# Multiplying the first dense layer once per token pair (k, S-k), with the sum and the difference formed on Vector

## The chip, the core and the metric

The kernel runs on one core of a Trainium2 chip. The metric is the device time of one execution in microseconds; the median of three executions of the kernel before is 3000.6 us (3000.43 to 3002.52). The engines are TensorE (PE in the profile, its weight loads PEld), Vector (DVE), Scalar (ACT), GpSimd (POOL) and Sync (SP). Data are float32; the two weight matrices arrive as 64-bit floats and are converted on Vector.

## The reference

```python
# x: (8, 3008, 256)   w_in: (256, 2048)   w_out: (2048, 256)
X = np.fft.fft(np.fft.fft(x, axis=1), axis=2).real     # over the sequence, then over d
x2 = X.reshape(8 * 3008, 256)
h = x2 @ w_in
g = h * np.clip(h + 3.0, 0.0, 6.0) / 6.0
out = g @ w_out                                         # (24064, 256)
```

## The kernel before

The sequence transform of length S = 3008 is split as 47 x 64 (N1, N2). Since x is real, only the residues k1 = 0..23 (NK1 = 24) are computed: the cosine part of a token k equals that of token S-k, the sine part has the opposite sign. Along d, x is first folded into sums x[d] + x[D-d] (columns 0 to D/2) and differences (the other columns), and the last product over d is multiplied into w_in once (fold_w_in, L268), so that h is a product of 256 rows: 128 of the cosine kind, 128 of the sine kind.

Batches go in four pairs. For a pair, eight rounds of load_x (L90, issued by GpSimd), fold (L95, three Vector instructions) and stage1 (L104, four calls a round: one product of 512 columns and one of two columns, which repairs column D/2 among the sine columns; Scalar copies the result out) write an intermediate to DRAM. load_g (L124) brings it back in pieces of eight k1 for one batch, and stage2 (L132, 16 passes of 64 columns a call, then a Vector copy) makes q, whose columns are tokens.

The dense layers run over chunks of up to 8 x 64 = 512 tokens of one batch (chunks_of, L152): 12 chunks a pair, namely for each batch three with the tokens k and three with their partners S-k (the last of these has 7 x 64 = 448). For the partners the same q is read backwards, and the sine block of the weights is the negated copy W1m1. Each chunk has 16 blocks of 128 hidden columns; a chunk and a block make one step, 4 x 12 x 16 = 768 steps. In a step mlp1 (L159) makes h by two products of 512 columns added in PSUM, Scalar makes t (L170), Vector the gate a (L172); mlp2 (L175) multiplies the four tiles of 128 tokens of a with w_out, 256 columns each, adding up in PSUM over the 16 blocks. After the last block Scalar copies each tile and Sync stores it in pieces of 64 tokens.

The order of the instructions is written by hand. mlp1 runs two steps ahead of mlp2 (AHEAD = 2, L333). What belongs to the next chunks and the next pair (load_x, fold, stage1, load_g, stage2, and in the first chunk the conversion of w_out) is placed by beside (L303) into slots of chunk and block; the slot's work is issued ahead of that step's mlp1 and mlp2. In each engine's queue the order is that of issue. PSUM has eight banks: two for stage1 and stage2 (ps_d), two for h (ps_h), four for the accumulators (ps_a), of which a chunk uses two.

Before the loop stand the first pair's eight rounds (L278), with the conversion of w_in and fold_w_in between them, the first batch's load_g and stage2, and two conversions of w_out (eight Vector instructions each, L230 to L237).

Of the kernel before, what the change touches and what calls it, by code (L numbers as in the profile page):

```python
# [27 lines left out]
def kernel(  # L28
# [37 lines left out]
    ps_h = ctx.enter_context(tc.tile_pool(name="ps_h", bufs=2, space=PSUM))  # L66
# [3 lines left out]
    out_k = out.rearrange("(b k2 k1) d -> b k1 k2 d", b=B, k1=N1)  # L70
# [3 lines left out]
    F = consts.tile([PR, 2, PZ], F32, name="F")  # L74
    T = consts.tile([P, 2, NK1, N2], F32, name="T")
    C = consts.tile([P, 2, D], F32, name="C")
    W1p = consts.tile([P, 2, FF], F32, name="W1p")
    W1m1 = consts.tile([P, FF], F32, name="W1m1")
    W2 = consts.tile([P, NFC, D], F32, name="W2")
    half = consts.tile([P, 1], F32, name="half")  # L80
    sign = consts.tile([P, 1], F32, name="sign")

    class Pair:
        def __init__(self, p):
            self.p = p
            self.x, self.y, self.z = {}, {}, {}
            self.zd = None
            self.g, self.q = {}, {}
# [6 lines left out]
    def fold(pr, c):  # L95
        xt = pr.x.pop(c)
        y = ypool.tile([PR, XC, D], F32, tag="y", name="y")
        lo, hi = xt[:, :, 1:P], xt[:, :, D - 1:P:-1]
        nc.vector.tensor_tensor(y[:, :, 1:P], lo, hi, op=AL.add)  # L99
        nc.vector.tensor_tensor(y[:, :, P + 1:D], lo, hi, op=AL.subtract)  # L100
        nc.vector.tensor_copy(y[:, :, 0:P + 1:P], xt[:, :, 0:P + 1:P])  # L101
        pr.y[c] = y
# [21 lines left out]
    def load_g(pr, b, kc):  # L124
        g = gpool.tile([P, KC, D], F32, tag="g", name="g")
        nc.gpsimd.dma_start(  # L126
            out=g[:],
            in_=pr.zd[b].rearrange("k c n d -> (c n) k d")[:, kc * KC:(kc + 1) * KC, :],
        )
        pr.g[b, kc] = g  # L130

    def stage2(pr, b, kc, i):  # L132
        if kc == 0 and i == 0:
            pr.q[b] = qpool.tile([P, 2, NK1, N2], F32, tag="q", name="q")
        g = pr.g[b, kc]
        ps = ps_d.tile([P, 2, 4, N2], F32, tag="d", name="ps2")
        for u in range(4):
            k1 = kc * KC + 4 * i + u
            for blk in range(2):
                nc.tensor.matmul(ps[:, blk, u], g[:, 4 * i + u, blk * P:(blk + 1) * P], T[:, blk, k1],  # L140
                                 start=True, stop=True)
        k0 = kc * KC + 4 * i
        nc.vector.tensor_copy(pr.q[b][:, :, k0:k0 + 4, :], ps[:])  # L143

    class Chunk:
        def __init__(self, pr, b, sg, k0, k1):
            self.pr, self.b, self.sg, self.k0, self.n = pr, b, sg, k0, k1 - k0
            self.nt = self.n * N2
            self.tiles = [(t, min(P, self.nt - t)) for t in range(0, self.nt, P)]
            self.a, self.acc = {}, {}  # L150

    def chunks_of(pr):  # L152
        for b in range(2):
            for sg in (1, -1):
                first = 0 if sg > 0 else 1
                for k0 in range(first, NK1, KC):
                    yield Chunk(pr, b, sg, k0, min(k0 + KC, NK1))

    def mlp1(ch, fc):  # L159
        q = ch.pr.q[ch.b]  # L160
        ps = ps_h.tile([P, TB], F32, tag="h", name="h")
        h = ps[:, 0:ch.nt]
# [6 lines left out]
        t = tpool.tile([P, TB], F32, tag="t", name="t")  # L169
        nc.scalar.activation(t[:, 0:ch.nt], h, AF.Relu, bias=half[:], scale=1.0 / 6.0)  # L170
        a = apool.tile([P, TB], F32, tag="a", name="a")
        nc.vector.scalar_tensor_tensor(a[:, 0:ch.nt], t[:, 0:ch.nt], 1.0, h, op0=AL.min, op1=AL.mult)  # L172
        ch.a[fc] = a

    def mlp2(ch, fc):  # L175
        a = ch.a.pop(fc)
        for i, (t0, n) in enumerate(ch.tiles):
# [3 lines left out]
            nc.tensor.matmul(ch.acc[i // 2][0:n, i % 2], a[:, t0:t0 + n], W2[:, fc, :],  # L181
                             start=(fc == 0 and i % 2 == 0), stop=(fc == NFC - 1), skip_group_check=True)
        if fc == NFC - 1:
            for i, (t0, n) in enumerate(ch.tiles):
                acc = ch.acc[i // 2]
                o = opool.tile([P, D], F32, tag="o", name="o")
                nc.scalar.copy(o[0:n], acc[0:n, i % 2])  # L187
                for j in range(n // N2):
                    k1 = ch.k0 + (t0 + j * N2) // N2
                    rows = out_k[2 * ch.pr.p + ch.b]  # L190
                    dst = rows[k1 if ch.sg > 0 else N1 - k1]
                    nc.sync.dma_start(out=dst, in_=o[j * N2:(j + 1) * N2])
# [9 lines left out]
    # The weights' pieces, [P, 512] each: a 64-bit one comes as pairs of 32-bit words, of  # L202
    # which the float32 is made here.
# [61 lines left out]
    nc.vector.memset(sign[:], -1.0)  # L265
    nc.vector.memset(sign[0:1], 1.0)

    def fold_w_in(n):  # L268
        cs = slice(n * 512, (n + 1) * 512)
        for blk in range(2):  # L270
            ps = ps_h.tile([P, 512], F32, tag="h", name="wps")
# [3 lines left out]
            nc.scalar.copy(W1p[:, blk, cs], ps[:])  # L275
        nc.vector.tensor_scalar(W1m1[:, cs], W1p[:, 1, cs], sign[:], None, op0=AL.mult)

    for c in range(NXC):  # L278
        if c + 2 < NXC:
            load_x(first, c + 2)  # L280
        fold(first, c)
# [9 lines left out]
    for kc in range(NKC):  # L291
        load_g(first, 0, kc)
        for i in range(KC // 4):
            stage2(first, 0, kc, i)
# [4 lines left out]
    # what runs beside the second part: slots of (chunk of the pair, f block)  # L299
    chunks = [list(chunks_of(pr)) for pr in pairs]  # L300
    NCK = len(chunks[0])

    def beside(p):  # L303
# [11 lines left out]
        for kc in range(NKC):  # L315
            put(kc, 0, load_g, cur, 1, kc)
            for i in range(KC // 4):
                put(kc + 1, 4 + 6 * i, stage2, cur, 1, kc, i)
# [83 lines left out]
```

## Time and profile before

| | |
|---|---|
| median of three runs | 3000.6 us |
| span of the profiled execution (first to last instruction) | 2998.8 us |
| TensorE busy | 2944.5 us (98%) |
| Vector busy | 692.9 us (23%) |
| Scalar busy | 663.4 us (22%) |
| GpSimd busy | 38.6 us (1%) |
| mean granted TensorE clock | 0.985 |

The profiled execution's own time is its span and what lies around it; the median of the runs is 1.8 us above that span. In the trace each float32 product appears as two passes, each with its own weight load, so a step's two products of 512 columns are four rows and its four products of 256 columns are eight. A matmul's row is longer than the distance to the next one because matmuls overlap; the distance from start to start is the time that counts. A granted clock of 1.00 is 2.4 GHz, half of it 1.2 GHz.

### The profile page before, as it was taken

What the parts mean: (1) busy time and instruction counts of PE and PEld (TensorE: products, weight loads), DVE (VectorE), ACT (ScalarE), POOL (GpSimd) and SP (SyncE); (2) the same over time, 40 slices, a digit from 0 to 9 for tenths busy, and PEclk for the clock granted to TensorE, in tenths of its full rate; (3) what the DMA queues carried; (4) which work ended last, traced back from release to release, by engine and by line L of the source; (5) the groups of instructions that cost most, each with busy time, mean ns of one, the idle gap of its engine ahead of it and who ended that gap; (6) DMA issues with size and microseconds to landing.
All of it is one profiled execution on the core that took longest, in us unless ns stands there. A gap on an engine that the chain in (4) does not pass through costs nothing.

```text
span 2998.8 us, 25017 instructions
## 1 busy us (share of the span) xinstructions
PE 2944.5 (98%) x10528; PEld 1896.6 (63%) x10528; DVE 692.9 (23%) x1047; ACT 663.4 (22%) x1097; POOL 38.6 (1%) x60
## 2 busy tenths in 40 slices
PE   6899999999999999999999999999999999999999
PEld 2556665666656666566666666566675666666665
DVE  4362222222212222122221222222121222112111
ACT  1122222222222222222212222222212222222221
POOL 0000000000000000000000000000000000000000
PEclk8699999999999999999999999999999999999999
DMA  6422111001200211002020211110111000000000
GB/s 190 150 62 63 28 28 40 23 18 50 69 11 8 69 33 45 17 18 59 26 56 7 60 39 28 28 28 25 46 36 27 8 21 8 15 7 8 14 8 14
DMA packets 47728, 111.53 MB, mean 37 GB/s; under 512 B 7778, under 2 KB 32192, under 8 KB 41408
## 3 DMA queue, kind: packets, MB, share of 16 engines
q1 hardware_dynamic: 37360, 58.56, 7.4%
q0 software_dynamic: 10112, 49.81, 5.7%
q8 instruction: 82, 1.34, 0.2%
q10 hardware_dynamic: 144, 1.57, 0.2%
q14 instruction: 30, 0.25, 0.0%
HBM read 60.10 MB, written 49.81 MB: 37 GB/s over the span
## 4 chain that ended last, share of the span: by engine, by line
PE 97%; DMA 1%; DVE 1%; issue 0%; ACT 0%; SPq 0%; ACTq 0%; POOLq 0%
PE acc L181 45%; PE h L168 44%; PE ps L113 4%; PE ps L140 3%; DMA st<-in_moe_w_in_dram 1%; PE wps L273 1%; DMA g<-zd 0%; PE ps L114 0%; DMA st<-in_moe_w_out_dram 0%; DVE y L99 0%; DVE y L100 0%; DVE ex L236 0%; DVE frac L232 0%; ACT W1p L275 0%; DVE top L230 0%
## 5 line engine op out<-in xcount | busy, mean ns | idle before, releaser
L181 PE MATMUL acc<-W,a 128*128 128x256 f32 (+1 forms) x6144 | 1470.9, 380 | 0.0
L181 PEld LDWEIGHTS acc<-W,a 128*128 128x128 f32 (+1 forms) x6144 | 1143.8, 188 | 509.2 <-issue 396.5
L168 PE MATMUL h<-q,W1p 128*128 128x512 f32 (+1 forms) x2304 | 1124.7, 597 | 5.5 <-DVE a L172 5.5
L172 DVE SCALAR_TENSOR_TENSOR a<-t,h 128x512 f32<-128x512 f32 (+1 forms) x768 | 519.6, 677 | 2116.9 <-ACT t L170 2116.9
L170 ACT ACTIVATE t<-h,half 128x512 f32<-128x512 f32 (+1 forms) x768 | 521.0, 678 | 2002.3 <-PE h L168 2002.3
L168 PEld LDWEIGHTS h<-q,W1p 128*128 128x128 f32 x2304 | 419.3, 190 | 262.1 <-issue 223.4
L168 PE MATMUL h<-q,W1m 128*128 128x512 f32 (+1 forms) x768 | 378.5, 574 | 0.0
L168 PEld LDWEIGHTS h<-q,W1m 128*128 128x128 f32 x768 | 145.9, 190 | 170.0 <-issue 170.0
L113 PE MATMUL ps<-y,F 94*96 94x512 f32 x256 | 159.1, 708 | 32.7 <-DMA F<-in_c_stage_dram 18.4
L116 ACT COPY z<-ps 96x512 f32<-96x512 f32 x128 | 74.4, 581 | 284.5 <-PE ps L114 284.5
L140 PEld LDWEIGHTS ps<-T,g 128*128 128x128 f32 x768 | 102.3, 209 | 12.8 <-issue 10.6
L140 PE MATMUL ps<-T,g 128*128 128x64 f32 x768 | 100.5, 290 | 9.6 <-issue 9.3
L114 PEld LDWEIGHTS ps<-y,F 94*96 94x96 f32 x256 | 48.4, 189 | 85.1 <-issue 85.1
L113 PEld LDWEIGHTS ps<-y,F 94*96 94x96 f32 x256 | 42.6, 187 | 45.7 <-issue 39.8
L187 ACT COPY o<-acc 128x256 f32<-128x256 f32 x192 | 62.0, 375 | 24.6 <-PE acc L181 24.6
L143 DVE COPY q<-ps 128x512 f32<-128x512 f32 x48 | 33.2, 692 | 112.1 <-PE ps L140 112.1
L126 POOL DMA_DIRECT2D g<-zd x24 | 21.4, 892 | 1670.1 <-PE ps L140 958.7
L99 DVE TENSOR_TENSOR y<-xt 94x1016 f32<-94x1016 f32 x32 | 38.6, 1205 | 9.8 <-DMA xt<-in_x_dram 9.8
L100 DVE TENSOR_TENSOR y<-xt 94x1016 f32<-94x1016 f32 x32 | 38.6, 1206 | 0.0
L114 PE MATMUL ps<-y,F 94*96 94x2 f32 x256 | 35.7, 209 | 0.0
L92 POOL DMA_DIRECT2D xt<-in_x_dram x32 | 17.1, 536 | 705.4 <-DVE y L101 704.6
L273 PE MATMUL wps<-w_in,C 128*128 128x512 f32 x32 | 22.5, 867 | 0.0
(21 smaller groups left out, 90.5 us busy)
## 6 DMA issues: line engine op xcount, KB each, us to landing
zd<-z SPq DMA_DIRECT2D x32, 768.0 KB, 4.3
g<-zd POOLq DMA_DIRECT2D x24, 1024.0 KB, 6.7
xt<-in_x_dram POOLq DMA_DIRECT2D x32, 752.0 KB, 7.9
out_dram<-o SPq DMA_DIRECT2D x376, 64.0 KB, 2.0
st<-in_moe_w_in_dram SPq DMA_DIRECT2D x8, 512.0 KB, 6.7
st<-in_moe_w_out_dram SPq DMA_DIRECT2D x8, 512.0 KB, 6.4
T<-in_c_stage_dram ACTq DMA_DIRECT2D x1, 1536.0 KB, 8.6
C<-in_c_dim_dram SPq DMA_DIRECT2D x1, 256.0 KB, 17.8
```

The lines of the kernel that those rows point to most:

```text
L99: nc.vector.tensor_tensor(y[:, :, 1:P], lo, hi, op=AL.add)
L100: nc.vector.tensor_tensor(y[:, :, P + 1:D], lo, hi, op=AL.subtract)
L113: nc.tensor.matmul(ps[0:PZ], F[:, 0], y[:, 2 * i:2 * i + 2, :], start=True, stop=True)
L114: nc.tensor.matmul(ps[0:PZ, :, P:P + 1], F[:, 1], y[:, 2 * i:2 * i + 2, P:P + 1], start=True, stop=True)
L116: nc.scalar.copy(z[:, 2 * i:2 * i + 2, :], ps[0:PZ])
L140: nc.tensor.matmul(ps[:, blk, u], g[:, 4 * i + u, blk * P:(blk + 1) * P], T[:, blk, k1], start=True, stop=True)
L168: nc.tensor.matmul(h, w, qc, start=(blk == 0), stop=(blk == 1))
L170: nc.scalar.activation(t[:, 0:ch.nt], h, AF.Relu, bias=half[:], scale=1.0 / 6.0)
L172: nc.vector.scalar_tensor_tensor(a[:, 0:ch.nt], t[:, 0:ch.nt], 1.0, h, op0=AL.min, op1=AL.mult)
L181: nc.tensor.matmul(ch.acc[i // 2][0:n, i % 2], a[:, t0:t0 + n], W2[:, fc, :], start=(fc == 0 and i % 2 == 0), stop=(fc == NFC - 1), skip_g ...
L187: nc.scalar.copy(o[0:n], acc[0:n, i % 2])
L273: nc.tensor.matmul(ps[:], C[:, i, blk * P:(blk + 1) * P], w_in[n, i][0][:], start=(i == 0), stop=(i == 1))
```

## The change

- The pairs of tokens k and S-k are computed together. mlp1 makes u (the cosine part) and v (the sine part) in two banks of PSUM, one product each. Vector forms s = u + (column D/2's term), then h0 = s + v for the tokens k and h1 = s - v, written backwards, for the tokens S-k. Scalar makes t for both, and Vector gates both in a function of its own (gate), which is issued after the next step's mlp1.
- Column D/2 of the folded data leaves the matrix products: its row of weights is kept as WN, its transform qn is made with a Vector product (stage2n_mul) and a TensorE product with a matrix of ones, which sums over partitions and leaves the sum in all of them (stage2n_sum); s adds WN times qn. In exchange the two-column product of stage1 goes, and fold_w_in gets eight products of one column for each of its four calls.
- A chunk is four k1 of both batches of the pair, so 6 chunks a pair and 384 steps; each has eight tiles of 128 tokens in mlp2 (seven in the last chunk of a pair). The k1 are taken in the order 1..23, 0.
- PSUM: u and v have one bank each; fold_w_in uses ps_d; a chunk uses all four banks of ps_a.
- The folds beside the loop run on GpSimd, in two parts; the copies of stage2 move from Vector to Scalar; x has two buffers instead of three, and before the loop the load of round c+2 is issued after the fold of round c. Only the first chunk's q is made before the loop. Two tiles are copied and stored together.

```diff
-        nc.tensor.matmul(ps[0:PZ], F[:, 0], y[:, 2 * i:2 * i + 2, :], start=True, stop=True)
-        nc.tensor.matmul(ps[0:PZ, :, P:P + 1], F[:, 1], y[:, 2 * i:2 * i + 2, P:P + 1],
-                         start=True, stop=True)
+        nc.tensor.matmul(ps[0:PZ], F[:], y[:, 2 * i:2 * i + 2, :], start=True, stop=True)
...
+    def stage2(pr, ck, i):
+        if i == 0:
+            pr.q[ck] = qpool.tile([P, 2, KC, N2], F32, tag="q", name="q")
+        g = pr.g[ck]
+        ps = ps_d.tile([P, 2, 4, N2], F32, tag="d", name="ps2")
+        for u in range(4):
+            kk, b = 2 * i + u // 2, u % 2
+            for blk in range(2):
+                nc.tensor.matmul(ps[:, blk, u], g[:, b, kk, blk * P:(blk + 1) * P],
+                                 T[:, blk, ck * KK + kk], start=True, stop=True)
+        nc.scalar.copy(pr.q[ck][:, :, 4 * i:4 * i + 4, :], ps[:])
+    def stage2n_mul(pr, ck):
+        m = spool.tile([P, KK, 2, N2], F32, tag="m", name="m")
+        t0 = T[:, 0, ck * KK:(ck + 1) * KK, :].unsqueeze(2).to_broadcast([P, KK, 2, N2])
+        gn = pr.g[ck][:, :, :, P:P + 1].rearrange("p b k o -> p k b o").to_broadcast([P, KK, 2, N2])
+        nc.vector.tensor_tensor(m[:], t0, gn, op=AL.mult)
+        pr.pr[ck] = m
+    def stage2n_sum(pr, ck):
+        m = pr.pr.pop(ck)
+        ps = ps_d.tile([P, TB], F32, tag="d", name="ps3")
+        nc.tensor.matmul(ps[:], ones[:], m[:].rearrange("p k b n -> p (k b n)"), start=True, stop=True)
+        pr.qn[ck] = qpool.tile([P, TB], F32, tag="qn", name="qn")
+        nc.scalar.copy(pr.qn[ck][:], ps[:])
...
-        ps = ps_h.tile([P, TB], F32, tag="h", name="h")
-        for blk in range(2):
-            w = W1m1[:, fs] if blk and ch.sg < 0 else W1p[:, blk, fs]
-            qc = q[:, blk, ch.k0:ch.k0 + ch.n, ::ch.sg]
-            nc.tensor.matmul(h, w, qc, start=(blk == 0), stop=(blk == 1))
-        nc.scalar.activation(t[:, 0:ch.nt], h, AF.Relu, bias=half[:], scale=1.0 / 6.0)
-        nc.vector.scalar_tensor_tensor(a[:, 0:ch.nt], t[:, 0:ch.nt], 1.0, h, op0=AL.min, op1=AL.mult)
+        u = ps_h.tile([P, TB], F32, tag="u", name="u")
+        v = ps_h.tile([P, TB], F32, tag="v", name="v")
+        nc.tensor.matmul(u[:], W1[:, 0, fs], q[:, 0], start=True, stop=True)
+        nc.tensor.matmul(v[:], W1[:, 1, fs], q[:, 1], start=True, stop=True)
+        s = spool.tile([P, KC, N2], F32, tag="s", name="s")
+        h = hpool.tile([P, 2, KC, N2], F32, tag="h", name="h")
+        t = hpool.tile([P, 2, KC, N2], F32, tag="t", name="t")
+        nc.vector.scalar_tensor_tensor(s[:].rearrange("p k n -> p (k n)"), qn[:], WN[:, fc:fc + 1], u[:],
+                                       op0=AL.mult, op1=AL.add)
+        nc.vector.tensor_tensor(h[:, 0], s[:], v3, op=AL.add)
+        nc.vector.tensor_tensor(h[:, 1, 0:nm, ::-1], s[:, 0:nm], v3[:, 0:nm], op=AL.subtract)
+        for sg, n in ((0, KC), (1, nm)):
+            nc.scalar.activation(t[:, sg, 0:n], h[:, sg, 0:n], AF.Relu, bias=half[:], scale=1.0 / 6.0)
+    def gate(ch, fc):
+        a = apool.tile([P, 2, KC, N2], F32, tag="a", name="a")
+        for sg, n in ((0, KC), (1, ch.nm)):
+            nc.vector.scalar_tensor_tensor(a[:, sg, 0:n], t[:, sg, 0:n], 1.0, h[:, sg, 0:n],
+                                           op0=AL.min, op1=AL.mult)
...
+            put(at_ck, 1, stage2n_mul, pr, ck)
+            for i in range(2):
+                put(at_ck, 3 + 4 * i, stage2, pr, ck, i)
+            put(at_ck, 11, stage2n_sum, pr, ck)
...
+                a0 = 8 * c
+                put(a0 // NFC, a0 % NFC, load_x, nx, c)
+                put((a0 + 3) // NFC, (a0 + 3) % NFC, fold, nx, c, 0, nc.gpsimd)
+                put((a0 + 4) // NFC, (a0 + 4) % NFC, fold, nx, c, 1, nc.gpsimd)
...
         if s + AHEAD < len(steps):
-            p1, ck1, fc1 = steps[s + AHEAD]
-            mlp1(chunks[p1][ck1], fc1)
-        mlp2(chunks[p][ck], fc)
+            mlp1(*chunk(s + AHEAD))
+        if s + 1 < len(steps):
+            gate(*chunk(s + 1))
+        mlp2(*chunk(s))
```

## Rows read from the trace of the kernel before

**Rows 1.** The page's busy times: engine, us, share, instructions.

```profile
PE 2944.5 (98%) x10528; PEld 1896.6 (63%) x10528; DVE 692.9 (23%) x1047; ACT 663.4 (22%) x1097; POOL 38.6 (1%) x60
```

**Rows 2.** Stretches: length, busy us of PE, PEld, DVE, ACT, POOL; clock, DMA share, GB/s.

```profile
18.36:115.80 97.44, 83.00 (x160) 35.57 (x160) 49.42 (x88) 22.72 (x40) 2.05 (x4) 0.74 0.51 144
...
160.00:2992.40 2832.40, 2832.40 (x10261) 1836.98 (x10259) 623.83 (x922) 636.79 (x1052) 28.44 (x41) 1.00 0.11 29
```

**Rows 3.** Timeline of a full step: start, length, engine, line, what, idle before.

```profile
2801.00 1.88 PE L168 MATMUL h<-q,W1p 128*128 128x512 f32 x4
...
2802.72 1.89 PE L181 MATMUL acc<-W,a 128*128 128x256 f32 x8
...
2802.92 0.69 ACT L170 ACTIVATE t<-h,half 128x512 f32<-128x512 f32 x1 [2.75 <-PE h L168]
2803.64 0.69 DVE L172 SCALAR_TENSOR_TENSOR a<-t,h 128x512 f32<-128x512 f32 x1 [2.76 <-ACT t L170]
...
2811.33 1.02 PE L168 MATMUL h<-q,W1p 128*128 128x512 f32 x2
```

**Rows 4.** Timeline, two steps of 448 tokens.

```profile
2977.49 1.02 PE L168 MATMUL h<-q,W1p 128*128 128x448 f32 x2
...
2981.06 1.02 PE L168 MATMUL h<-q,W1p 128*128 128x448 f32 x2
```

**Rows 5.** Timeline of TensorE, a stage2 and a stage1 call in the loop.

```profile
227.94 1.89 PE L140 MATMUL ps<-T,g 128*128 128x64 f32 x16
229.68 1.94 PE L168 MATMUL h<-q,W1p 128*128 128x512 f32 x4
...
236.62 1.02 PE L113 MATMUL ps<-y,F 94*96 94x512 f32 x2
237.48 0.25 PE L114 MATMUL ps<-y,F 94*96 94x2 f32 x2
237.59 1.96 PE L168 MATMUL h<-q,W1p 128*128 128x512 f32 x4
```

**Rows 6.** Groups by line and shape: busy us, mean ns | idle before, releaser.

```profile
L172 DVE SCALAR_TENSOR_TENSOR a<-t,h 128x512 f32<-128x512 f32 x640 | 440.1, 688 | 1743.1 <-ACT t L170 1743.1
L170 ACT ACTIVATE t<-h,half 128x512 f32<-128x512 f32 x640 | 439.9, 687 | 1671.6 <-PE h L168 1671.6
...
L116 ACT COPY z<-ps 96x512 f32<-96x512 f32 x128 | 74.4, 581 | 284.5 <-PE ps L114 284.5
...
L99 DVE TENSOR_TENSOR y<-xt 94x1016 f32<-94x1016 f32 x32 | 38.6, 1205 | 9.8 <-DMA xt<-in_x_dram 9.8
```

**Rows 7.** Timeline of TensorE before and at the start of the loop.

```profile
18.36 1.99 PE L113 MATMUL ps<-y,F 94*96 94x512 f32 x2 [18.36 <-DMA F<-in_c_stage_dram]
...
47.53 1.07 PE L113 MATMUL ps<-y,F 94*96 94x512 f32 x2 [3.63 <-DVE y L101]
...
100.08 2.00 PE L113 MATMUL ps<-y,F 94*96 94x512 f32 x2
101.88 0.37 PE L114 MATMUL ps<-y,F 94*96 94x2 f32 x2
...
110.22 5.53 PE L273 MATMUL wps<-w_in,C 128*128 128x512 f32 x8
125.00 13.88 PE L140 MATMUL ps<-T,g 128*128 128x64 f32 x64 [9.25 <-issue]
...
159.86 2.83 PE L181 MATMUL acc<-W,a 128*128 128x256 f32 x8
```

**Rows 8.** Timeline of Vector, from the first conversion of w_out to the first gates.

```profile
146.98 0.77 DVE L230 TENSOR_SCALAR top<-st 128x512 int32<-128x512 int32 x1
...
155.55 1.28 DVE L172 SCALAR_TENSOR_TENSOR a<-t,h 128x512 f32<-128x512 f32 x2
```

**Rows 9.** DMA issues: count, KB each, median us from issue to landing.

```profile
xt<-in_x_dram POOLq DMA_DIRECT2D x32, 752.0 KB, 7.9
out_dram<-o SPq DMA_DIRECT2D x376, 64.0 KB, 2.0
```

**Rows 10.** Timeline, the last instruction before the end of the span at 2998.8.

```profile
2992.45 0.63 ACT L187 COPY o<-acc 128x256 f32<-128x256 f32 x2 [0.36 <-PE acc L181]
```

More of the change, by code (lines that the diff above doesn't have):

```diff
@@ L87, in __init__ @@
             self.zd = None
-            self.g, self.q = {}, {}
+            self.g, self.q, self.qn, self.pr = {}, {}, {}, {}
     def load_x(pr, c):
@@ L93, in load_x, with fold @@
         pr.x[c] = xt
-    def fold(pr, c):
-        xt = pr.x.pop(c)
-        y = ypool.tile([PR, XC, D], F32, tag="y", name="y")
+    def fold(pr, c, part, eng):
+        if part == 0:
+            pr.y[c] = ypool.tile([PR, XC, D], F32, tag="y", name="y")
+        xt, y = pr.x[c], pr.y[c]
         lo, hi = xt[:, :, 1:P], xt[:, :, D - 1:P:-1]
[L99 to L102, printed above, removed]
+        if part == 0:
+            eng.tensor_tensor(y[:, :, 1:P], lo, hi, op=AL.add)
+        else:
+            eng.tensor_tensor(y[:, :, P + 1:D], lo, hi, op=AL.subtract)
+            eng.tensor_copy(y[:, :, 0:P + 1:P], xt[:, :, 0:P + 1:P])
+            del pr.x[c]
     def stage1(pr, c, i):
@@ L122, in stage1, with load_g @@
             del pr.y[c], pr.z[c]
[L124 to L135, printed above, removed]
+    def load_g(pr, ck):
+        g = gpool.tile([P, 2, KK, D], F32, tag="g", name="g")
+        for b in range(2):
+            nc.gpsimd.dma_start(
+                out=g[:, b],
+                in_=pr.zd[b].rearrange("k c n d -> (c n) k d")[:, ck * KK:(ck + 1) * KK, :],
+            )
+        pr.g[ck] = g
@@ L176, in mlp2, with store @@
         a = ch.a.pop(fc)
-        for i, (t0, n) in enumerate(ch.tiles):
+        last = fc == NFC - 1
+        for i, (sg, j) in enumerate(ch.tiles):
             if fc == 0 and i % 2 == 0:
                 ch.acc[i // 2] = ps_a.tile([P, 2, D], F32, tag="acc", name="acc")
[L181 to L192, printed above, removed]
+            nc.tensor.matmul(ch.acc[i // 2][:, i % 2],
+                             a[:, sg, 2 * j:2 * j + 2, :].rearrange("p k n -> p (k n)"), W2[:, fc, :],
+                             start=(fc == 0 and i % 2 == 0), stop=last, skip_group_check=True)
+            if last and (i % 2 == 1 or i == len(ch.tiles) - 1):
+                store(ch, i // 2)
+    def store(ch, m):
+        ts = ch.tiles[2 * m:2 * m + 2]
+        o = opool.tile([P, 2, D], F32, tag="o", name="o")
+        nc.scalar.copy(o[:, 0:len(ts)], ch.acc[m][:, 0:len(ts)])
+        ks = [(ch.ck * KK + j + 1) % NK1 for _, j in ts]
+        ks = [N1 - k if sg else k for (sg, _), k in zip(ts, ks)]
+        for b in range(2):
+            rows = out_k[2 * ch.pr.p + b]
+            src = o[b * N2:(b + 1) * N2]
+            if len(ks) == 2 and abs(ks[1] - ks[0]) == 1:
+                st = ks[1] - ks[0]
+                nc.sync.dma_start(out=rows[:, ks[0]:ks[0] + 2 * st:st, :], in_=src)
+            else:
+                for r, k in enumerate(ks):
+                    nc.sync.dma_start(out=rows[:, k:k + 1, :], in_=src[:, r:r + 1])
     pairs = [Pair(p) for p in range(NP)]
@@ L264 @@
     nc.vector.memset(half[:], 0.5)
-    nc.vector.memset(sign[:], -1.0)
-    nc.vector.memset(sign[0:1], 1.0)
+    nc.gpsimd.memset(ones[:], 1.0)
     def fold_w_in(n):
@@ L274, in fold_w_in @@
                                  start=(i == 0), stop=(i == 1))
-            nc.scalar.copy(W1p[:, blk, cs], ps[:])
-        nc.vector.tensor_scalar(W1m1[:, cs], W1p[:, 1, cs], sign[:], None, op0=AL.mult)
+            nc.scalar.copy(W1[:, blk, cs], ps[:])
+        ps = ps_d.tile([P, 512], F32, tag="d", name="wns")
+        for j in range(512 // P):
+            for i in range(2):
+                nc.tensor.matmul(ps[:, j:j + 1], w_in[n, i][0][:, j * P:(j + 1) * P], C[:, i, D:D + 1],
+                                 start=(i == 0), stop=(i == 1))
+        nc.scalar.copy(WN[:, n * (512 // P):(n + 1) * (512 // P)], ps[:, 0:512 // P])
     for c in range(NXC):
+        for part in range(2):
+            fold(first, c, part, nc.vector)
         if c + 2 < NXC:
             load_x(first, c + 2)
-        fold(first, c)
         for i in range(XC // 2):
@@ L290 @@
         load_w_out(j)
[L291 to L294, printed above, removed]
+    load_g(first, 0)
+    load_g(first, 1)
+    for i in range(2):
+        stage2(first, 0, i)
+    stage2n_mul(first, 0)
+    stage2n_sum(first, 0)
     for j in range(2):
@@ L297 @@
         load_w_out(j + 2)
-    chunks = [list(chunks_of(pr)) for pr in pairs]
-    NCK = len(chunks[0])
+    chunks = [[Chunk(pr, ck) for ck in range(NCK)] for pr in pairs]
     def beside(p):
@@ L314, in beside, with s2 @@
                     put(0, 2 * j - 3, load_w_out, j + 2)
[L315 to L318, printed above, removed]
+        def s2(at_ck, pr, ck):
+            put(at_ck, 1, stage2n_mul, pr, ck)
+            for i in range(2):
+                put(at_ck, 3 + 4 * i, stage2, pr, ck, i)
+            put(at_ck, 11, stage2n_sum, pr, ck)
+        for ck in range(1, NCK):
+            if ck > 1:
+                put(ck - 2, 12, load_g, cur, ck)
+            s2(ck - 1, cur, ck)
         if p + 1 < NP:
@@ L333, with chunk @@
     AHEAD = 2
-    for s in range(AHEAD):
+    def chunk(s):
         p, ck, fc = steps[s]
-        mlp1(chunks[p][ck], fc)
+        return chunks[p][ck], fc
+    mlp1(*chunk(0))
+    mlp1(*chunk(1))
+    gate(*chunk(0))
     for s, (p, ck, fc) in enumerate(steps):
```

87 lines of the change are left out of this document (39 added, 48 removed).

## The prediction

> **What bounds the kernel now.** I read the busy times first: TensorE is busy for 2944.5 of 2998.8 us, Vector for 23% and Scalar for 22% [rows 1]. A busy share alone says little for pipelined matmuls, so I looked next at one step of the main loop in the order of time [rows 3]. Four passes of 512 columns (each float32 product is two passes in the trace) start at 2801.00, the eight passes of the second layer at 2802.72, and three steps later the picture repeats at 2811.33: 3.443 us a step, 1.72 us for each layer, with no gap. Scalar and Vector rows there show idle time of 2.75 us ahead of each 0.69 us instruction: they wait for TensorE and never the reverse. The stretch table says the same of the whole: from 160 to 2992.4 us TensorE is busy for all 2832.4 us, at a granted clock of 1.00, the 2.4 GHz level [rows 2].
>
> Does counting explain that stretch? There are 768 steps. The 640 full ones take 3.443 us each, 2203.5 us. The 128 with 448 tokens take 3.57 us (2977.49 to 2981.06), more than the full ones though they hold fewer tokens [rows 4]: 457.0 us. Between them lie 96 calls of stage1 at 0.97 us (236.62 to 237.59) and 42 of stage2 at 1.74 us (227.94 to 229.68) [rows 5], 166.2 us. The sum is 2826.7 us. The measured time is from the first second-layer product at 159.86 [rows 7] to 2992.4, 2832.5 us, plus 5.2 us for the first layers of three steps done before it: 2837.7. The 11 us left over are 0.08 us for each of the 138 insertions. So the loop is the sum of TensorE's passes, and a change pays what it takes from that sum, as long as nobody else gets late.
>
> **The main loop after the change.** There are 4 pairs x 6 chunks x 16 = 384 steps. Each holds two products of 512 columns (u and v, four passes, 1.72 us) for 1024 tokens instead of 512, and eight second-layer tiles, 2 x 1.72 us: 5.165 us. The last chunk of each pair has seven tiles, all of 128 tokens, 1.72 x 2.75 = 4.735 us; the slow 448-token step goes. The sum is 64 x (5 x 5.165 + 4.735) = 1956 us against 2660.5 now.
>
> Between the steps: 96 calls of stage1 without the two-column product (236.62 to 237.48, 0.86 us) are 82.6 us; 46 calls of stage2 at 1.74 us (four of the six that stood before the loop move into it) are 80.0 us; 23 products with the matrix of ones, two passes of 512 columns, 0.86 us each, 19.8 us; 0.08 us for each of these 165 insertions, 13.2 us. Together 196 us. So the loop is 2152 us, 2147 from the first second-layer product on, less 685 than now.
>
> **What has to stay hidden: Vector and Scalar.** Vector goes from one instruction to five per step (s, sum, difference, two gates). None of these exact forms is in the trace. From below: 0.61 us, the spacing that back-to-back rows of 512 elements come near (the two instructions from 155.55 end after 1.28 us) [rows 8]. From above: 1.205 us, the fold over 1016 elements, one operand read backwards [rows 6]. I take 0.688 us, the row of the present gate (512 elements, one operand in PSUM) [rows 6], as it is the nearest. Five are 3.44 us of a 5.165 us step. The stage2n product adds one such instruction in one step of sixteen, and the copies of stage2 leave Vector for Scalar. Scalar has two activations of 0.687 us and at most two copies of about 0.6 us [rows 6], 2.6 us.
>
> Order matters more than sums. u and v have one bank each now. In one step, counted from the start of u: u ends at 0.86, v at 1.72; s runs from about 1.1 to 1.8, sum and difference end at 3.3 (the 0.2 us between product and reader as in [rows 3]), the gates of the step before end at 4.7. TensorE comes back to u at 5.17 and to v at 6.03, when both banks have long been read, and needs those gates only at 6.9. So there are 2.2 us of cover on the gate and 1.7 us of free Vector time per step. If that cover were gone, each 0.1 us over would cost 38 us. At a chunk's end all four accumulator banks are in use where two were free before: the four copies (some 0.65 us each) begin after the activations at about 4.0 in Scalar's queue when counted with their own 0.69 us, the first bank is wanted at 6.9, the later ones 0.86 us apart. I cost it at nothing.
>
> In the first chunk Vector also converts the second weights, six times in every second step. Two such conversions took 8.57 us (146.98 to 155.55) [rows 8], so 4.3 us each: 4.3 + 2 x 3.44 = 11.2 us of Vector against 10.3 of TensorE. Over six of them, less the 1.7 to 2.2 us of cover, 4 us come through. Bounds: 0 (0.61 us an instruction) and 12.
>
> **Folds on GpSimd.** The 24 folds beside the loop leave Vector (2.6 us each, two of 1.205 and a small copy). No row shows GpSimd computing. It has a load before it three steps ahead (15 us, against 7.9 for a load of x [rows 9]) and its reader four steps behind; its queue also holds the g loads, each wanted five steps (26 us) or more later, three before the pair's end. Up to three times Vector's 2.6 us all that stays hidden. I take nothing; the upper bound is the rival below.
>
> A rule of the Trainium skill speaks against this part: the GPSIMD Engine Reference, Key points, says that GpSimd shares its SBUF interfaces with Vector and that they contend where Vector's instruction has two SBUF inputs, which the two gates here have. No run here shows it yet. The same page's section When to use GPSIMD calls it about 2x slower for two inputs.
>
> **Before the loop.** Now the first stage1 product waits until 18.36 us [rows 7], while the queues bring x. With two x buffers instead of three, one load of 0.75 MB leaves this opening and F is half as large; I take 16 us (bounds 13 to 18.4). Eight rounds follow at a mean clock of 0.74 [rows 2], mostly at the 1.2 GHz level: a pair of passes takes 1.80 us (100.08 to 101.88), twice the 0.86 of [rows 5]. Two rounds are 8 x 1.80 = 14.4 us, plus 5.6 for folding w_in (110.22, 5.53), plus the new 16 passes for column D/2; the nearest rows are stage2's, 64 passes in 13.88 us, 0.217 each, 3.5 us. The wait of 3.63 us for Vector (47.53) goes, since Vector no longer scales W1m1 there. That gives 23.5 us for two rounds, 94 for eight, so 110 us, and the last stage1 product ends at 101. From there g took 14.8 us to arrive (110.22 to 125.00): 116. Two stage2 calls, 6.9 us, and the ones product with its copy, 2.6 us, bring u(0) to 125.5; Vector has its two conversions done by then. Two steps' s, sum and difference and the first gates, one after the other, with u and v of one buffer each: some 9.5 us. The first second-layer product starts at 135 us instead of 159.86.
>
> **The end.** 6.4 us lie behind the last product now, with four copies and seven stores; after the change it is one copy, started before most stores have gone, and two stores of 2.0 us [rows 9, 10]. I take 4 us.
>
> Sum: 135 + 2147 + 4 + 4 = 2290 us of span; the medians lie 1.8 us above the profile's span, so 2292; taking the 0.61 us spacing as likely for part of Vector's first chunk, I round to 2288.
>
> **Rivals.**
> 1. The opening runs at the higher clock. Without the two-column products the passes of stage1 follow each other. Rows at either level: 1.80 or 0.86 us per call. Then two rounds cost 6.9 + 3.5 + 1.8 = 12.2 us on TensorE and 14 on Vector (two folds of 2.6, two conversions of 4.3), which becomes their bound: 57 us instead of 94, the loop starts near 98, and the time is 2250. For it: the w_in products, eight back to back, shorten within their 5.5 us. Against: stage1 stays low for 8 us at a stretch now. The Trainium skill (TensorE: Matmul & The Clock Gate, What's actually happening) says that recent activity releases the throttle; the rows agree in direction.
> 2. GpSimd and Vector hinder each other: a fold stops the gates beside it for as long as it lasts. With one to three times Vector's 2.6 us for a fold, 2.6 to 7.8 us less the 1.7 to 2.2 us of cover come through, 24 times: 10 to 146 us. The middle, 5.2 us a fold, leaves 3 us x 24 = 72: 2360. For it: gates read two operands from SBUF. Against: cover, and that Vector's own folds now run beside Scalar and TensorE without any change of pace.
> 3. Vector becomes the bound: from 1.03 us per instruction on (5.165 / 5). With the 1.205 us of the fold's row a step is 6.0 us, 2314 us for 384, and with the opening 2455. Against: rows of 512 elements with a PSUM operand all lie near 0.69 [rows 3, 6].
> 4. Slower than before: the look-ahead fails, and each step's second layer waits for its own gate, since u, v are single. A step is then 1.72 + 0.69 x 4 (sum, difference, activation, gate) + 3.44 + 0.3 for the handovers = 8.2 us, 384 x 8.2 = 3150, with the opening 3290. It decides from (2999 - 143 - 196) / 384 = 6.93 us per step on. Against: the order of issue puts gate(s+1) a whole second layer ahead of its reader, as counted above.
>
> **Chances.** Forecast, 2265 to 2305: 0.55. Rival 1, 2235 to 2265: 0.2. Rival 2, 2305 to 2360: 0.15. Rival 3: 0.06. Rival 4: 0.04. The range 2240 to 2335 leaves out some 2 in 10: the ends of rivals 1 and 2, and 3 and 4 whole. Faster by over 0.2% (what a measurement here can tell from no change): 0.96; within it 0.01; slower 0.03.
>
> **What would show it.** In the changed profile: 5.16 us between successive u products and no idle time of TensorE ahead of them; about 2250 us TensorE busy; Vector near 60% and Scalar near 30%; the second layer's groups unchanged at 0.215 us a pass; the first layer's count halved. Idle time on TensorE released by Vector would show rival 3 or 4, gates that are longer in stretches with folds rival 2, stage1 calls of 0.86 us before 100 us rival 1. The forecast is wrong if a step in mid-loop lasts over 5.3 us.

## The result and the profile after

The changed kernel takes 2265.8 us (median of four runs, 2261.74 to 2266.62) against 3000.9: a ratio of 0.7546, 95% interval 0.7536 to 0.7557. The forecast was 2288 us with a range of 2240 to 2335. The profiled execution has a span of 2263.3 us where 2290 were summed.

The page's busy times after the change, to be read against [rows 1]:

```profile
PE 2217.8 (98%) x8720; PEld 1591.3 (70%) x8720; DVE 1389.2 (61%) x2097; ACT 675.2 (30%) x1077; POOL 181.4 (8%) x157
```

TensorE lost 727 us of work and is still busy for 98% of the span; Vector's time doubled, to 61% of the span (near 60% in the forecast), and it did not become the bound. One step in the middle of the loop, from the timeline (start, length, engine, line, what, idle before), answers to [rows 3]:

```profile
1901.07 1.02 PE L182 MATMUL u<-q,W 128*128 128x512 f32 x2
...
1901.93 1.02 PE L183 MATMUL v<-q,W 128*128 128x512 f32 x2
...
1902.13 0.75 DVE L189 SCALAR_TENSOR_TENSOR s<-qn,WN,u 128x512 f32<-128x512 f32 x1 [1.83 <-PE u L182]
...
1902.79 3.62 PE L213 MATMUL acc<-W,a 128*128 128x256 f32 x16
...
1902.99 0.69 DVE L191 TENSOR_TENSOR h<-s,v 128x512 f32<-128x512 f32 x1
1903.59 0.68 DVE L193 TENSOR_TENSOR h<-s,v 128x512 f32<-128x512 f32 x1
1903.77 1.33 ACT L195 ACTIVATE t<-h,half 128x512 f32<-128x512 f32 x2 [3.84 <-DVE h L191]
1904.19 1.29 DVE L202 SCALAR_TENSOR_TENSOR a<-t,h 128x512 f32<-128x512 f32 x2
...
1906.24 1.02 PE L182 MATMUL u<-q,W 128*128 128x512 f32 x2
```

From u to u are 5.17 us, against 5.165 in the sum. TensorE's rows carry no idle time. Vector waits 1.83 us for u in each step, and its last gate ends at 1905.48, 4.41 us after u began (4.7 in the forecast).

The stretches (length, busy us of PE, PEld, DVE, ACT, POOL with counts, granted clock, DMA share, GB/s) show where the forecast was less good, the opening. Its eight rounds ran at a clock of 0.95 between 16 and 80 us, against 0.74 over the eight rounds in [rows 2]; from 130 to 2240 us TensorE is busy without a gap:

```profile
16.00:80.00 64.00, 59.93 (x160) 25.05 (x158) 48.58 (x85) 23.81 (x43) 2.58 (x5) 0.95 0.79 229
80.00:130.00 50.00, 31.75 (x94) 20.61 (x95) 38.87 (x54) 7.26 (x12) 16.86 (x15) 0.73 0.57 172
130.00:2240.00 2110.00, 2110.00 (x8405) 1533.20 (x8404) 1292.29 (x1943) 638.34 (x1013) 159.77 (x129) 1.00 0.14 39
```

TensorE's timeline of the opening answers to [rows 7]:

```profile
15.61 7.11 PE L122 MATMUL ps<-y,F 94*96 94x512 f32 x8 [15.61 <-DMA F<-in_c_stage_dram]
...
31.18 4.25 PE L314 MATMUL wps<-w_in,C 128*128 128x512 f32 x8
35.27 1.84 PE L320 MATMUL wns<-C,w_in 128*128 128x1 f32 x16
36.97 7.25 PE L122 MATMUL ps<-y,F 94*96 94x512 f32 x16
...
54.75 5.51 PE L122 MATMUL ps<-y,F 94*96 94x512 f32 x8 [1.77 <-DVE y L111]
...
108.28 3.62 PE L213 MATMUL acc<-W,a 128*128 128x256 f32 x16
118.71 2.08 PE L182 MATMUL u<-q,W 128*128 128x512 f32 x2 [6.81 <-DVE s L189]
...
122.28 4.79 PE L213 MATMUL acc<-W,a 128*128 128x256 f32 x16
```

The first two rounds of stage1 take 7.11 us for eight passes each, the lower level; the next two take 7.25 us for sixteen, the upper one. The clock column misses this at the start: it reads 1.00 from 16 to 31 us, where these slow passes run, and 1.00 from 18.4 to 42 us of the kernel before, where a stage1 product lasts 2.0 us. Both means, 0.95 and 0.74, are therefore too high, and the spacing of the passes is the better witness. The first second-layer product starts at 108.28 us instead of the 135 forecast. The second comes 14.0 us later instead of 5.17: TensorE waits 6.81 us for Vector. On Vector's and GpSimd's timeline the reason stands beside it:

```profile
107.94 2.43 POOL L108 TENSOR_TENSOR y<-xt 94x1016 f32<-94x1016 f32 x1 [6.40 <-DMA xt<-in_x_dram]
108.09 2.56 DVE L271 TENSOR_SCALAR top<-st 128x512 int32<-128x512 int32 x1
...
110.58 3.98 DVE L272 TENSOR_SCALAR low<-st 128x512 int32<-128x512 int32 x1
111.90 2.36 POOL L110 TENSOR_TENSOR y<-xt 94x1016 f32<-94x1016 f32 x1
```

Two instructions of a conversion, 0.42 us each elsewhere, last 2.56 and 3.98 us; each ends 0.3 us after a part of GpSimd's fold does (110.37 and 114.26).

Of the 735 us gained, 685 lie between the first second-layer product and the last product's end (2832.5 us before, 2147.5 after), and 51.6 ahead of that stretch; the end is 1.2 us longer.

### The profile page after: what moved, and what is told of

It reads as the page before. It is cut to its first block, busy times and chain, and to the rows that moved or that the text cites. A ratio compares the mean times of both kernels' runs of the same rounds, so it can differ in the third digit from the quotient of the medians.

```text
span 2263.3 us, 22686 instructions
## 1 busy us (share of the span) xinstructions
PE 2217.8 (98%) x8720; PEld 1591.3 (70%) x8720; DVE 1389.2 (61%) x2097; ACT 675.2 (30%) x1077; POOL 181.4 (8%) x157
## 3 DMA queue, kind: packets, MB, share of 16 engines
q10 hardware_dynamic: 144, 1.57, 0.2%
## 4 chain that ended last, share of the span: by engine, by line
PE 97%; DVE 2%; DMA 1%; issue 0%; ACT 0%; SPq 0%; POOL 0%; ACTq 0%; DVEq 0%
PE acc L213 57%; PE u L182 15%; PE v L183 15%; PE ps L122 5%; PE ps L149 4%; PE ps L164 1%; DMA st<-in_moe_w_in_dram 1%; PE wps L314 1%; DMA g<-zd 0%; DMA st<-in_moe_w_out_dram 0%; PE wns L320 0%; DVE low L272 0%; DVE ex L277 0%; DVE ex L276 0%; DVE top L271 0%; DVE frac L273 0%
## 5 line engine op out<-in xcount | busy, mean ns | idle before, releaser
L213 PEld LDWEIGHTS acc<-W,a 128*128 128x128 f32 x6016 | 1143.9, 190 | 319.7 <-issue 181.2
L213 PE MATMUL acc<-W,a 128*128 128x256 f32 x6016 | 1362.1, 379 | 0.0
L189 DVE SCALAR_TENSOR_TENSOR s<-qn,WN,u 128x512 f32<-128x512 f32 x384 | 286.9, 747 | 778.4 <-PE u L182 778.4
L182 PE MATMUL u<-q,W 128*128 128x512 f32 x768 | 397.2, 598 | 10.4 <-DVE s L189 10.4
L183 PE MATMUL v<-q,W 128*128 128x512 f32 x768 | 394.0, 595 | 0.4 <-DVE h L193 0.4
L191 DVE TENSOR_TENSOR h<-s,v 128x512 f32<-128x512 f32 x384 | 264.2, 688 | 43.4 <-PE v L183 1.3
L183 PEld LDWEIGHTS v<-q,W 128*128 128x128 f32 x768 | 145.8, 190 | 186.4 <-issue 105.0
L193 DVE TENSOR_TENSOR h<-s,v 128x512 f32<-128x512 f32 (+1 forms) x384 | 252.7, 658 | 0.0
L182 PEld LDWEIGHTS u<-q,W 128*128 128x128 f32 x768 | 142.8, 191 | 84.6 <-issue 60.7
L108 POOL TENSOR_TENSOR y<-xt 94x1016 f32<-94x1016 f32 x24 | 56.3, 2345 | 973.7 <-PE ps L122 927.0
L110 POOL TENSOR_TENSOR y<-xt 94x1016 f32<-94x1016 f32 x24 | 57.4, 2393 | 0.1
```

The costliest lines, as they stand in the source:

```text
L110: eng.tensor_tensor(y[:, :, P + 1:D], lo, hi, op=AL.subtract)
L182: nc.tensor.matmul(u[:], W1[:, 0, fs], q[:, 0], start=True, stop=True)
L183: nc.tensor.matmul(v[:], W1[:, 1, fs], q[:, 1], start=True, stop=True)
L189: nc.vector.scalar_tensor_tensor(s[:].rearrange("p k n -> p (k n)"), qn[:], WN[:, fc:fc + 1], u[:], op0=AL.mult, op1=AL.add)
L191: nc.vector.tensor_tensor(h[:, 0], s[:], v3, op=AL.add)
L193: nc.vector.tensor_tensor(h[:, 1, 0:nm, ::-1], s[:, 0:nm], v3[:, 0:nm], op=AL.subtract)
```

## The experiments

Where a ratio is given, the time is the median of four to six executions. The other experiments are one execution each; the four of the changed kernel differ by up to 4.9 us.

**The first layer's passes doubled.** The question is whether the loop is really the sum of TensorE's passes.

```diff
-        nc.tensor.matmul(u[:], W1[:, 0, fs], q[:, 0], start=True, stop=True)
-        nc.tensor.matmul(v[:], W1[:, 1, fs], q[:, 1], start=True, stop=True)
+        for _ in range(2):
+            nc.tensor.matmul(u[:], W1[:, 0, fs], q[:, 0], start=True, stop=True)
+            nc.tensor.matmul(v[:], W1[:, 1, fs], q[:, 1], start=True, stop=True)
```

> The changed kernel with the products u and v made twice in each step, so that the first layer has as many passes as before the change. Theory A (the loop is the sum of TensorE's passes): 384 x 1.72 = 661 us more, 2927 us, no idle time of TensorE in the loop. Rival B (part of the loop's time has another bound that hides TensorE work): clearly less, under 2850 us.

Measured: 2920.6 us, 654.8 more than the changed kernel. The timeline shows 6.88 us a step, and from 135 to 2890 us TensorE is busy for all 2755.0 us:

```profile
2500.15 1.02 PE L183 MATMUL u<-q,W 128*128 128x512 f32 x2
...
2507.03 1.02 PE L183 MATMUL u<-q,W 128*128 128x512 f32 x2
```

Theory A holds; the 6 us that are missing lie at the start, where the added passes fill waits that are there anyhow. So by this run the first layer's halving is worth some 655 of the 735 us.

**The half tile of the kernel before.** The sum took the 448-token step at its measured 3.57 us without an explanation. This run leaves the 64-token tile out (its second layer and its stores).

```diff
-            self.tiles = [(t, min(P, self.nt - t)) for t in range(0, self.nt, P)]
+            self.tiles = [(t, P) for t in range(0, self.nt // P * P, P)]
```

> The kernel before without the tile of 64 tokens that ends each chunk of 448 (its second layer and its stores are left out, so those rows of the output are not written). It tells what the half tile costs that the change does away with. Theory A (the half tile costs more than its passes, because it disturbs those next to it): the step falls from 3.57 to what full passes predict, 4 x 0.376 for 448 columns + 6 x 0.215 = 2.80 us; 128 x 0.77 = 99 us less, 2902 us. Rival B (it costs its two passes): 3.57 - 0.43 = 3.14 us, 55 us less, 2946.

Measured: 2903.1 us, 98 less than before, with 2.80 us a step in the timeline:

```profile
2861.44 0.92 PE L168 MATMUL h<-q,W1p 128*128 128x448 f32 x2
2862.19 0.92 PE L168 MATMUL h<-q,W1m 128*128 128x448 f32 x2
2862.94 1.46 PE L181 MATMUL acc<-W,a 128*128 128x256 f32 x6
...
2864.24 0.92 PE L168 MATMUL h<-q,W1p 128*128 128x448 f32 x2
```

In the kernel before, the same place reads:

```profile
2976.91 0.65 PE L181 MATMUL acc<-W,a 128*64 128x256 f32 x2
2977.49 1.02 PE L168 MATMUL h<-q,W1p 128*128 128x448 f32 x2
2978.35 0.92 PE L168 MATMUL h<-q,W1m 128*128 128x448 f32 x2
```

Theory A: two passes with 64 stationary columns (the tile's tokens) cost 0.77 us a step, where two full passes of 256 columns are 0.43. Of the other 0.34, 0.15 is in the two passes themselves, 0.58 us from start to start (2976.91 to 2977.49). Another 0.11 is in the passes behind them: with the half tile in the step, the first two passes of the first layer take 0.86 us from start to start (2977.49 to 2978.35) for 448 columns, without it 0.75. The change does not gain all of the 98 us: 64 full tiles of 0.43 us take the place of the 128 half tiles, which leaves some 71.

**No look-ahead.** This is the forecast's fourth rival made real.

```diff
-    mlp1(*chunk(0))
-    mlp1(*chunk(1))
-    gate(*chunk(0))
...
-        if s + AHEAD < len(steps):
-            mlp1(*chunk(s + AHEAD))
-        if s + 1 < len(steps):
-            gate(*chunk(s + 1))
+        mlp1(*chunk(s))
+        gate(*chunk(s))
         mlp2(*chunk(s))
```

> The changed kernel without look-ahead: in each step u and v, the gates and the second layer are issued one behind the other. Theory A (the order of issue is what hides Vector and Scalar): TensorE waits 3.06 us for the gates in each step (from v's end to the end of the second gate in the changed kernel's rows), 8.24 us a step, 384 x 8.24 + 196 + 104 = 3465 us at the 2.4 GHz level, more if the clock falls: slower than before the change. Rival B (the waits overlap in another way, for instance by buffers alone): under 3000 us.

Measured: 3761.5 us. The order alone decides whether the change gains 25% or loses 25%. TensorE's timeline:

```profile
3007.82 1.02 PE L182 MATMUL u<-q,W 128*128 128x512 f32 x2
3008.68 1.02 PE L183 MATMUL v<-q,W 128*128 128x512 f32 x2
3012.02 5.41 PE L213 MATMUL acc<-W,a 128*128 128x256 f32 x16 [2.32 <-DVE a L202]
3017.26 1.02 PE L182 MATMUL u<-q,W 128*128 128x512 f32 x2
```

A step is 9.44 us, 1.2 more than counted, and two errors stand behind that. The wait is shorter than counted: the second layer starts 2.48 us after v's passes (3009.54 to 3012.02), not 3.06, since it begins as soon as the first of the two gates is done. But then it takes 5.24 us instead of 3.45, because the granted clock fell: 0.67 in this stretch, 0.867 in the mean of the run.

**Two and four more Vector instructions a step.** How much cover is there?

```diff
-        nc.vector.tensor_tensor(h[:, 0], s[:], v3, op=AL.add)
+        for _ in range(3):       # 5 in the other run
+            nc.vector.tensor_tensor(h[:, 0], s[:], v3, op=AL.add)
```

> The changed kernel with the sum h0 formed three times in each step (the same values), two Vector instructions more, some 1.2 us at the spacing of 0.6 us in the changed kernel's rows; Vector then needs 4.55 of 5.17 us. Theory A (TensorE sets the step, Vector has 1.8 us to spare and the gates 2.2 us of cover; folds on GpSimd stop the gates for some 1.6 us each): the last pair, without folds, keeps 5.17 us a step; in stretches with folds up to 1 us comes through per fold, and some 12 us in the first chunk: 2278 to 2305 us. Rival B (Vector already sets the step): 1.2 x 384 = 460 us more, 2725.

> As the run with two more, with four more Vector instructions a step (h0 formed five times): Vector needs 3.35 + 2.4 = 5.75 us of a step that TensorE ends in 5.17. Theory A: Vector becomes the bound, 5.75 us a step also in the last pair, 384 x 0.58 = 223 us and more where folds stop it: 2490 to 2560 us, TensorE idle ahead of u by waits for Vector. Rival B (Vector's time adds up in full): 2.4 x 384 = 920 us more, 3190.

Measured: 2278.2 us with two more, 2599.2 with four more. With two more, a step of the last pair still takes 5.17 us (2000.85 to 2006.02), Vector's wait for u has shrunk from 1.83 to 0.38 us, and from 200 to 2250 us TensorE is busy without a gap, folds and all. The 12 us lie in the first chunk (8.4 us of TensorE's idle time between 130 and 200 us; by 130 us some 2 more were lost), so what was expected to come through at the folds, up to 1 us each, did not. With four more the step is set by Vector:

```profile
1984.51 1.02 PE L182 MATMUL u<-q,W 128*128 128x512 f32 x2
1986.41 1.10 PE L183 MATMUL v<-q,W 128*128 128x512 f32 x2 [0.89 <-DVE h L194]
1987.35 3.19 PE L214 MATMUL acc<-W,a 128*128 128x256 f32 x14
1990.37 1.02 PE L182 MATMUL u<-q,W 128*128 128x512 f32 x2
```

These steps have seven tiles and take 5.86 us where TensorE alone needs 4.74. Steps of eight tiles take some 6.14 us (2293.50 to 2299.64) instead of the expected 5.75, since sums written to the same place start 0.72 us apart (three in 2.13 us), not 0.6: over 320 such steps some 125 us, enough to bring the total above the expected 2490 to 2560.

**The folds on Vector again.**

```diff
-                put((a0 + 3) // NFC, (a0 + 3) % NFC, fold, nx, c, 0, nc.gpsimd)
-                put((a0 + 4) // NFC, (a0 + 4) % NFC, fold, nx, c, 1, nc.gpsimd)
+                put((a0 + 3) // NFC, (a0 + 3) % NFC, fold, nx, c, 0, nc.vector)
+                put((a0 + 4) // NFC, (a0 + 4) % NFC, fold, nx, c, 1, nc.vector)
```

> The changed kernel with the 24 folds beside the loop on Vector again instead of GpSimd. Theory A (a Vector instruction that uses both of its SBUF reads stands still while GpSimd works): the waits of TensorE at the start of the loop (3.6 and 6.8 us for Vector's s) shrink, the conversions of w_out there go back to 0.42 and 0.69 us per instruction, no gate lasts over 0.8 us; time 2256 to 2263 us. Rival B (Vector's own load decides, GpSimd is harmless): the 2.6 us of each fold come on top in the first chunk, 2267 to 2275 us.

Measured: 2255.8 us, ratio to before 0.7519 (0.7507 to 0.7532), faster than the change as given (0.7536 to 0.7557). Theory A: moving the folds to GpSimd cost 10 us. The wait ahead of the second step falls from 6.81 to 1.33 us, and the conversion goes back to its old pace:

```profile
107.26 1.12 PE L182 MATMUL u<-q,W 128*128 128x512 f32 x2 [1.33 <-DVE s L189]
```

```profile
102.36 0.42 DVE L271 TENSOR_SCALAR top<-st 128x512 int32<-128x512 int32 x1
102.69 0.42 DVE L272 TENSOR_SCALAR low<-st 128x512 int32<-128x512 int32 x1
```

The gates by their line (shortest, median and longest in ns), in the changed kernel and in this run:

```profile
L202 DVE SCALAR_TENSOR_TENSOR a<-t,h x768: 549/685/3908, 106.9 to 2249.5; 128x512 f32<-128x512 f32 x192
```

```profile
L202 DVE SCALAR_TENSOR_TENSOR a<-t,h x768: 548/684/686, 101.2 to 2237.2; 128x512 f32<-128x512 f32 x192
```

The longest of the 768 gates lasts 0.686 us here and 3.908 us with the folds on GpSimd; the sums s and h, with one operand in PSUM, never exceed 0.749 us in either.

**What set the clock of the opening.** Three runs. The first puts a product of two columns behind each stage1 product of the first pair:

```diff
+        if pr is first:
+            nc.tensor.matmul(ps[0:PZ, :, P:P + 1], F[:], y[:, 2 * i:2 * i + 2, P:P + 1],
+                             start=True, stop=True)
```

> The changed kernel with a product of two columns behind each stage1 product of the first pair (it writes the same values again). Theory A (the opening became shorter because stage1's passes now follow each other, and the clock rises to its upper level): the granted clock of 15 to 80 us falls to about 0.75, stage1 calls last 2 us, the first second-layer product comes at 120 to 135 us instead of 108; time 2278 to 2293. Rival B (the opening is set by loads and by Vector, which no longer scales the weights): only the products themselves come on top, 32 x 0.11 to 0.23 us = 4 to 7 us, the clock stays; time 2266 to 2273.

Measured: 2268.8 us, and a clock of 0.92 between 16 and 80 us. Rival B: the dense row of passes is not the reason; the 3 us more than the changed kernel are within what executions differ by. The second puts the scaling of the folded weights back on Vector, behind each w_in product:

```diff
         nc.scalar.copy(WN[:, n * (512 // P):(n + 1) * (512 // P)], ps[:, 0:512 // P])
+        w = wpool.tile([P, 512], F32, tag="top", name="scaled")
+        nc.vector.tensor_scalar(w[:], W1[:, 1, cs], -1.0, None, op0=AL.mult)
```

> The changed kernel with a scaling of the folded weights put back on Vector behind each of the four w_in products of the opening (its output is not used). Theory A (this wait is what dropped the clock): TensorE idles 2 to 4 us before the rounds 3, 5 and 7, the clock of 16 to 80 us falls from 0.95 to under 0.85, the first second-layer product comes at 118 to 132 us instead of 108, time 2276 to 2290. Rival B: 4 x 0.5 us of Vector, time 2264 to 2270, clock as it was. In the loop both theories see no difference.

Measured: 2282.7 us, clock 0.76 between 16 and 80 us, first second-layer product at 128.92. TensorE's timeline:

```profile
30.25 4.58 PE L314 MATMUL wps<-w_in,C 128*128 128x512 f32 x8
34.67 1.84 PE L320 MATMUL wns<-C,w_in 128*128 128x1 f32 x16
38.41 13.55 PE L122 MATMUL ps<-y,F 94*96 94x512 f32 x16 [1.90 <-DVE y L111]
```

The sixteen passes that took 7.25 us behind the same products take 13.55 us here; an idle stretch of 1.90 us ahead of them, behind the one-column products, is the difference. All eight rounds, with the folding of w_in, take 86.8 us (14.64 to 101.47), against 64.5 in the changed kernel (15.61 to 80.10) and 97.4 in the kernel before. The third takes the scaling's wait out of the kernel before, alone:

```diff
         fold(first, c)
+        if c and c % 2 == 0:
+            scale_w_in(c // 2 - 1)     # was the last line of fold_w_in
...
+    scale_w_in(NXC // 2 - 1)
```

> The kernel before, with one thing moved: in the opening, Vector scales W1m1 behind the next round's fold instead of ahead of it (the part of the change that takes this wait away, alone). Theory A (the opening of the kernel before ran at the lower clock because TensorE stood idle for 3.6 us behind each of the w_in products, waiting for Vector): the granted clock of 18 to 116 us rises from 0.74 to over 0.9, the first second-layer product comes at 120 to 135 us instead of 160, time 2965 to 2980. Rival B (only the waits themselves go, the clock stays): 3 x 3.6 = 11 us, time 2988 to 2992, clock 0.74 to 0.8.

Measured: 2990.9 us, ratio to before 0.9965 (0.9953 to 0.9978). The time is rival B's, and theory A's 2965 to 2980 us was missed; the clock, 0.81 over 18 to 116 us, is just above rival B's range. It rises no further for a visible reason:

```profile
43.79 1.02 PE L113 MATMUL ps<-y,F 94*96 94x512 f32 x2
44.77 1.08 PE L113 MATMUL ps<-y,F 94*96 94x512 f32 x2
...
51.70 1.99 PE L113 MATMUL ps<-y,F 94*96 94x512 f32 x2 [3.71 <-DVE y L101]
53.72 2.00 PE L113 MATMUL ps<-y,F 94*96 94x512 f32 x2
```

The round behind the w_in products now runs at the upper level, but it ends so early that the next fold is late by 3.7 us, and the round after that wait runs at the lower one again. The wait was moved, not removed. So the run bears out the cause, since the round behind a wait runs at the lower level and the round without one does not, but the expected gain did not come.

**A better start.** With the folds on Vector, two conversions go ahead of the wait for g, and T is loaded behind the third round.

```diff
-    nc.scalar.dma_start(out=T[:], in_=c_stage2)
...
+        if c == 2:
+            nc.scalar.dma_start(out=T[:], in_=c_stage2)
...
+    for j in range(2):
+        narrow_w_out(j)
+        load_w_out(j + 2)
     load_g(first, 1)
     for i in range(2):
         stage2(first, 0, i)
     stage2n_mul(first, 0)
     stage2n_sum(first, 0)
-    for j in range(2):
-        narrow_w_out(j)
-        load_w_out(j + 2)
```

> The changed kernel with the folds on Vector (as in the run above), the first two conversions of w_out issued ahead of the wait for g, and the load of T issued behind the third round. Theory A (what is left to gain lies ahead of the steady loop: x and F land sooner without T's 1.5 MB, and Vector uses its 13 us of waiting for g): the first stage1 product at 11 to 13 us instead of 14.5, no wait of TensorE for Vector in the first steps, time 2246 to 2253 us against 2256 with the folds alone moved. Rival B (Vector and loads bound the opening however T is placed, and the conversions were hidden already): 2254 to 2258 us.

Measured: 2254.4 us, ratio 0.7511 (0.7501 to 0.7522), not to be told from the run with the folds alone moved. Stage1 does start at 11.33 us, but TensorE then waits 5.99 us for a fold at 54.21, and the loop starts at 103.58 against 102.32: rival B. The fold stands in Vector's queue behind a conversion that waits 5.93 us for its piece of w_in at 47.51 (2.07 us at the same place in the run with the folds alone moved), with T's load, issued at 35.71, now ahead of it: Vector and the loads bound the rounds. Both versions beat the kernel before and the change as given.

## Why the prediction was right, and where it was not

- **The loop.** Right. It was forecast at 2147 us from the first second-layer product plus 4 us for the first chunk; from 108.28 to the last product's end (2246.52 + 9.23) are 2147.5 us. Inside, two errors cancel, which is luck. The 0.08 us for each insertion held for stage2 only: a stage1 call between two steps costs 0.86 us and nothing more (286.56 to 292.59 is 5.17 + 0.86), so the surcharge went with the two-column product, 96 x 0.08 = 8 us too much. The first chunk lost some 10 us (8.8 at the second step, 1.2 at the third) instead of 4.
- **Cover on Vector and Scalar.** Right: no idle time of TensorE from 130 us on, five Vector instructions in 3.5 us (0.747 + 0.688 + 0.680 + 2 x 0.685), and room for two more per step.
- **Folds on GpSimd at nothing.** Wrong at the start of the loop, right after it. They last 2.35 and 2.39 us a part, twice Vector's 1.205, and hold up Vector's gates and conversions until a part ends; the cover absorbs this in mid-loop (the run with two more instructions shows how safely), and not where the first conversions fill Vector. Rival 2 named this mechanism; it cost 10 us, the lower end of its 10 to 146. The Trainium skill's rule (GPSIMD Engine Reference, Key points), which names two SBUF inputs and the two-port mode as what contends, agrees with the trace: gates stretch, to 3.908 us, and s and h with their PSUM operand do not, 0.749 at most. The conversions' instructions with one input stretch too; that they run in the two-port mode no run here shows.
- **The opening.** The term that was mis-sized: 135 us forecast, 108.3 measured. The step that failed is the choice of the lower clock for all eight rounds: with the folding of w_in they were put at 94 us and took 64.5. Rival 1 had this right, and its sign came, stage1 calls near 0.86 us before 100 us (sixteen passes, eight calls, in 7.25 us). The time, 2265.8 us, lies between the forecast's 2288 and rival 1's 2250; that it falls into the forecast's own 2265 to 2305 is luck, by 0.8 us. Rival 1's reason was not the one at work: putting two-column products between the passes again changed 3 us of time and little of the clock. The wait of TensorE for Vector behind each w_in product had kept the clock down, and the forecast priced that wait at its own 3.63 us alone. The run with the scaling put back returns 22.3 of the 32.9 us that the rounds gained. The rest of the 51.6 us lies ahead of the rounds (2.8) and behind them (15.9, where two stage2 calls stand instead of six); these parts were not tried apart. The Trainium skill (TensorE: Matmul & The Clock Gate, HAM oscillation — how this bites in real kernels) describes kernels that lose their clock in waits between bursts of products; the run with the scaling put back agrees in direction, 0.76 against 0.95.
- **The end.** 7.6 us (2255.75 to 2263.3) against 4. Scalar has copied everything by 2256.2, but Sync issues its ten last stores one behind the other until 2260.6.

```profile
2254.24 1.13 SPq L230 DMA_DIRECT2D out_dram<-o  x2
...
2255.35 0.86 ACT L222 COPY o<-acc 128x512 f32<-128x512 f32 x2 [0.28 <-PE acc L213]
2255.47 2.46 SPq L233 DMA_DIRECT2D out_dram<-o  x4
2258.03 1.29 SPq L230 DMA_DIRECT2D out_dram<-o  x2
2259.41 1.20 SPq L233 DMA_DIRECT2D out_dram<-o  x2
```

- **The slower rival.** It was a fair one: without the order of issue the same arithmetic takes 3761 us. Its 3290 was too low for two reasons. The sum left out the 196 us between the steps, which the forecast counts elsewhere. And its step was under-priced (8.2 against 9.4 us) for the same reason as the opening, a wait that also costs clock: the wait was put too long, 3.06 us against 2.48, but the second layer behind it takes 5.24 us instead of 3.44.

## What to carry to other kernels

Where TensorE is busy without gaps, count its passes from start to start, and read odd shapes from their own rows: a tile of half width cost 0.77 us here, more than a full tile's 0.43. A wait of TensorE costs more than its length when the clock falls behind it, so price it at both levels of the clock. Work moved to GpSimd is not free for Vector; look for the place where Vector has no cover left.

## What the hardware showed that was not expected

- An idle stretch of 1.90 us, behind products of one column, was enough to lose the upper clock for the next 13.55 us of stage1 products; in the changed kernel, without it, the same sixteen passes took 7.25 us. In the changed kernel itself, 1.77 us of idle time behind a round at the upper level made the next eight passes last 5.51 us (from 54.75), where the eight before took 3.71.
- A Vector instruction of 0.42 us lasted up to 3.98 us beside GpSimd's folds, longer than the fold's part that it met: GpSimd issued the two DMAs for g between the parts (1.57 us from 110.32), and the row of Vector spans that too. Which of the two held it was not tried apart.
- Two passes with 64 stationary columns take longer than two with 128, 0.58 us against 0.43, and slow the passes next to them by another 0.19 us a step.
